# Chunked attention with a channel mix on one Trainium2 core: another way to load and turn the first q and k, three tiles mixed on PE, and a new order of the start

## The chip, the core and the metric

The kernel runs on one core of a Trainium2 chip. Its engines are TensorE (PE), VectorE (DVE), ScalarE (ACT), GpSimd (POOL) and the DMA queues, which SyncE (SP) and ScalarE issue to. The metric is the device time of one execution in microseconds: 616.96 us, the median of three runs (616.75 to 618.72).

## What is computed

The attention works in chunks of 64 tokens, so no chunk sees another one. Its output, 8 batches of 576 tokens of 512 channels, is the x of a channel mix, in which every token is blended with the one before it:

```python
scores = scale * np.matmul(q_c, k_c.transpose(0, 1, 2, 4, 3))   # chunks of 64 tokens, 8 heads of 64
attn = np.exp(scores - max) / (sum + 1e-09)
x = np.matmul(attn, v_c)                                       # to (8, 576, 512)
x_prev = np.concatenate([zeros, x[:, :-1, :]], axis=1)
xk = mu_k * x + (1.0 - mu_k) * x_prev
xr = mu_r * x + (1.0 - mu_r) * x_prev
k = np.maximum(xk @ w_k, 0.0)                                  # 512 -> 1024
v = k * k @ w_v                                                # 1024 -> 512
r = 1.0 / (1.0 + np.exp(-(xr @ w_r)))                          # 512 -> 512
out = r * v
```

q, k and v are float32; the three weight matrices and both mu come from numpy and the weights arrive as 8-byte floats, which the kernel converts on the chip.

## The kernel before

The 4608 tokens are worked in 18 groups of 256 (`G`), a group in two tiles of 128 (`TT`). For a tile, PE forms the scores (task `S`, line 363) from `qT` and `kT`, which hold channels on partitions; DVE and ACT make the softmax; PE turns the probabilities (task `P`, line 420) and multiplies them with v (line 438), which gives x with channels on partitions. Then x is mixed with its shifted self (tasks `Mk` and `Mr`) and split into a high and a low float32r part. For a group PE forms pk in four quarters (task `K`, line 580), pr for two tiles (`R`, line 629) and pv (`V`, line 659), each as three float32r passes (high by high, low by high, high by low). That is 96, 24 and 48 products a group.

From group 3 on q and k come in 32 by 32 blocks, which DVE turns. The first three groups, tiles 0 to 5, are loaded with a token a partition, 256 bytes to a head: `load_nat` issues for each tile and tensor one DMA for each half of the heads (`n` tasks, line 165; four where a tile crosses a batch). PE turns them, four products of 128 by 128 with the identity for a tile and tensor (task `T`, line 318), and ACT or DVE copies the result to `qT` or `kT` (line 131 or 133).

Of these first tiles, 0 to 3 (`ON_PE`, line 474) are mixed on PE: 16 products of x with diagonal matrices of mu and 1 - mu, accumulated (line 528). `make_diag` builds the 16 diagonals on ACT (line 489) from mu, loaded with channels on partitions in runs of 4 bytes (lines 216 and 217). The other tiles are mixed on DVE: a difference, then eight scalar_tensor_tensor instructions (line 540).

The weights come in ten pieces of 1 MB: w_r in two, w_k and w_v in four each. A piece takes two passes on ACT (lines 258 and 262), two on DVE (lines 265 and 271), a copy of the high part (line 131 on ACT or 133 on DVE) and a subtraction for the low part (line 280).

The order of the first two groups is written out by hand: `START` lists steps as task and number, with the engine behind a colon, and each engine and each DMA queue runs its own steps in this order. `W:14` puts 14 products of a zero tile in front of PE (line 723). From group 2 on `GROUP` gives the order. A DMA's end is told by one of eight semaphores, taken in turn, and the DMA that takes a semaphore again first waits for the DMA that had it before; the wait stands in the queue of the engine that issues it.

Of the kernel before, what the change touches and what calls it, by code (L numbers as in the profile page):

```python
# [7 lines left out]
F32 = mybir.dt.float32  # L8
# [3 lines left out]
AF = mybir.ActivationFunctionType  # L12
ALU = mybir.AluOpType
# [65 lines left out]
def tile_chunk_attention_channel_mix(  # L79
# [12 lines left out]
    nc = tc.nc  # L92
# [44 lines left out]
    def queue(e):  # L137
        return nc.scalar if e == "A" else nc.sync
# [7 lines left out]
    def segments(first, many):  # L146

        cut = -first % S
        if 0 < cut < many:
            return [(0, cut), (cut, many - cut)]  # L150
        return [(0, many)]

    def load_nat(t):
        for nm, src in (("q", q), ("k", k)):
            do.task = f"n{nm}{t}"

            def fn(_, nm=nm, src=src):
                g, tl = divmod(t, 2)
                if tl == 0:
                    T[f"{nm}{g}"] = ld.tile([P, 2, HP, 2, D], F32, tag=nm, name=f"{nm}n_{g}")  # L160
                dst = T[f"{nm}{g}"]
                for s, n in segments(t * TT, TT):
                    b, t0 = divmod(t * TT + s, S)
                    for j in range(2):
# [306 lines left out]

    ON_PE = (0, 1, 2, 3)
    diag = {}

    def make_diag():
        do.task = "dg"

        def fn(e):  # L480
            T["diag"] = tmp.tile([P, 4, NB, P], F32, tag="st", name="diag", bufs=1)
            for i, (nm, mu) in enumerate((("k", muk), ("r", mur))):
                rest = const.tile([P, NB], F32, name=f"rest{nm}")
                nc.vector.tensor_scalar(rest, mu, -1.0, 1.0, ALU.mult, ALU.add)
                for n, col in enumerate((mu, rest)):
                    to = diag[nm, n] = T["diag"][:, 2 * i + n]
# [12 lines left out]
    def x_mix(t):
# [16 lines left out]

        do(f_d, "D")
        for nm, mu in (("k", muk), ("r", mur)):

            def f_mix(e, nm=nm, mu=mu):  # L520
                x = xt[t]
                if t in ON_PE:
# [272 lines left out]
```

## Time and profile before

| what | value |
|---|---|
| median of three runs | 616.96 us |
| the profiled execution | 620.49 us, of which the span is 618.7 us |
| PE busy | 601.6 us, 97% |
| DVE busy, ACT busy | 399.8 us, 332.5 us |
| DMA | 49.17 MB, mean 79 GB/s |
| granted PE clock | 0.988 of full speed over the span |

The page cuts the span into 40 slices. PE is busy nine tenths or more from the fifth slice on; in the first four it shows 5, 8, 8 and 8 tenths, the PE clock 9, 7, 9 and 8 tenths. The DMA engines are busiest in those slices. A matmul's end is modelled, so that a lone product looks longer than the distance at which products follow each other. A float32 product with 128 columns stands in the trace as two instructions, a transpose as one.

### The profile page before, as it was taken

What the parts mean: (1) busy time and instruction counts of PE and PEld (TensorE: products, weight loads), DVE (VectorE), ACT (ScalarE), POOL (GpSimd) and SP (SyncE); (2) the same over time, 40 slices, a digit from 0 to 9 for tenths busy, and PEclk for the clock granted to TensorE, in tenths of its full rate; (3) what the DMA queues carried; (4) which work ended last, traced back from release to release, by engine and by line L of the source; (5) the groups of instructions that cost most, each with busy time, mean ns of one, the idle gap of its engine ahead of it and who ended that gap; (6) DMA issues with size and microseconds to landing.
All of it is one profiled execution on the core that took longest, in us unless ns stands there. A gap on an engine that the chain in (4) does not pass through costs nothing.

```text
span 618.7 us, 14035 instructions
## 1 busy us (share of the span) xinstructions
PE 601.6 (97%) x5676; PEld 529.2 (86%) x5676; DVE 399.8 (65%) x860; ACT 332.5 (54%) x519; POOL 0.7 (0%) x6
## 2 busy tenths in 40 slices
PE   5888999999999999999999999999999999999997
PEld 5778988989898989888888888898989898989895
DVE  2767879757666667666666666666766667675610
ACT  4767684454545464646463737372728282827250
POOL 0000000000000000000000000000000000000000
PEclk9798999999999999999999999999999999999999
DMA  8796343244233434242322442234233334020000
GB/s 190 219 280 172 105 109 78 43 88 94 36 56 75 105 70 85 52 90 48 75 52 39 90 98 34 56 79 103 34 62 68 74 77 83 19 57 13 18 18 34
DMA packets 195071, 49.17 MB, mean 79 GB/s; under 512 B 186816, under 2 KB 186816, under 8 KB 195008
## 3 DMA queue, kind: packets, MB, share of 16 engines
q1 hardware_dynamic: 193952, 48.29, 34.9%
q8 instruction: 44, 0.72, 0.5%
q10 hardware_dynamic: 1056, 0.00, 0.1%
q14 instruction: 19, 0.16, 0.1%
HBM read 38.80 MB, written 9.44 MB: 78 GB/s over the span
## 4 chain that ended last, share of the span: by engine, by line
PE 91%; DMA 4%; SPq 3%; DVE 1%; issue 0%; ACT 0%; DVEq 0%
PE pk L580 33%; PE pv L659 33%; PE pr L629 16%; PE xps L438 3%; PE s L363 3%; DMA wk_st<-in_moe_w_k 3%; PE pt L420 2%; SPq L165 2%; SPq L182 1%; DMA wr_st<-in_moe_w_r 1%; PE mxk L528 1%; PE mxr L528 0%; SPq L254 0%; DVE wk_st L265 0%; DVE wk L280 0%
## 5 line engine op out<-in xcount | busy, mean ns | idle before, releaser
L580 PE MATMUL pk<-xkhi,wk 128*128 128x256 f32 x1152 | 217.9, 285 | 1.9 <-DVE wk L133 1.1
L659 PE MATMUL pv<-wv,kk 128*128 128x512 f32 x864 | 205.4, 395 | 0.0
L659 PEld LDWEIGHTS pv<-wv,kk 128*128 128x128 f32 x864 | 161.4, 187 | 39.2 <-DVE wv L280 0.2
L580 PEld LDWEIGHTS pk<-xkhi,wk 128*128 128x128 f32 x1152 | 181.3, 189 | 4.2 <-DVE wk L133 1.3
L580 PE MATMUL pk<-xklo,wk 128*128 128x256 f32 x576 | 162.3, 282 | 0.0
L580 PEld LDWEIGHTS pk<-xklo,wk 128*128 128x128 f32 x576 | 109.3, 190 | 0.9
L594 ACT ACTIVATE relu<-pk 128x512 f32<-128x512 f32 x72 | 42.6, 592 | 99.3 <-PE pk L580 99.3
L613 DVE TENSOR_TENSOR kk<-relu,kk 128x512 fp32r<-128x512 f32 x72 | 49.5, 687 | 69.9 <-ACT kk L131 69.9
L629 PE MATMUL pr<-wr,xrhi 128*128 128x512 f32 x288 | 93.7, 406 | 0.0
L629 PEld LDWEIGHTS pr<-wr,xrhi 128*128 128x128 f32 x288 | 51.4, 188 | 11.0
L629 PE MATMUL pr<-wr,xrlo 128*128 128x512 f32 x144 | 56.8, 395 | 0.0
L373 DVE TENSOR_REDUCE m<-s 128x8 f32<-128x512 f32 x36 | 24.7, 687 | 47.8 <-PE s L363 47.8
L131 ACT ACTIVATE xkhi<-mixk 128x512 fp32r<-128x512 f32 x32 | 20.2, 632 | 58.2 <-DVE mixk L540 58.2
L131 ACT ACTIVATE xrhi<-mixr 128x512 fp32r<-128x512 f32 x31 | 19.6, 632 | 57.0 <-DVE mixr L540 57.0
L131 ACT ACTIVATE kk<-relu 128x512 fp32r<-128x512 f32 x72 | 45.6, 633 | 2.1
L601 ACT ACTIVATE relu<-relu 128x512 f32<-128x512 f32 x72 | 45.5, 632 | 2.1
L540 DVE SCALAR_TENSOR_TENSOR mixk<-d,muk,x 128x128 f32<-128x128 f32 (+1 forms) x144 | 38.5, 332 | 1.0
L540 DVE SCALAR_TENSOR_TENSOR mixr<-d,mur,x 128x128 f32<-128x128 f32 (+1 forms) x144 | 38.3, 331 | 0.0
L559 DVE TENSOR_TENSOR xrlo<-mixr,xrhi 128x512 fp32r<-128x512 f32 x32 | 22.2, 692 | 21.0 <-ACT xrhi L131 21.0
L559 DVE TENSOR_TENSOR xklo<-mixk,xkhi 128x512 fp32r<-128x512 f32 x32 | 22.1, 692 | 20.9 <-ACT xkhi L131 20.9
L672 DVE TENSOR_TENSOR out<-pv,sg 128x512 f32<-128x512 f32 x36 | 24.0, 675 | 16.7 <-PE pv L659 15.7
L131 ACT ACTIVATE pT<-pt 128x512 f32<-128x512 f32 x36 | 21.3, 591 | 22.6 <-PE pt L420 22.6
(75 smaller groups left out, 562.9 us busy)
## 6 DMA issues: line engine op xcount, KB each, us to landing
v<-in_v SPq DMA_DIRECT2D x144, 64.0 KB, 2.5
out<-out SPq DMA_DIRECT2D x36, 256.0 KB, 2.2
q<-in_q SPq DMA_DIRECT2D x160, 32.0 KB, 2.0
k<-in_k SPq DMA_DIRECT2D x160, 32.0 KB, 2.0
wk_st<-in_moe_w_k SPq DMA_DIRECT2D x4, 1024.0 KB, 8.1
wv_st<-in_moe_w_v SPq DMA_DIRECT2D x4, 1024.0 KB, 7.2
wr_st<-in_moe_w_r SPq DMA_DIRECT2D x2, 1024.0 KB, 8.1
qn<-in_q SPq DMA_DIRECT2D x10, 128.0 KB, 2.9
```

The lines of the kernel that those rows point to most:

```text
L131: nc.scalar.activation(to, x, AF.Copy)
L363: nc.tensor.matmul(scores()[halves[e], j, hp, :], qT[halves[j], hp, cols[e]], kT[halves[j], hp, cols[e]], start=True, stop=True,)
L373: nc.vector.tensor_reduce(out=heads(m), in_=scores(), axis=AX.X, op=ALU.max)
L540: nc.vector.scalar_tensor_tensor(out=m[:, cb, s : s + w], in0=d[:, cb, s : s + w], scalar=mu[:, cb : cb + 1], in1=x[:, cb, c : c + w], op0 ...
L559: engine[e].tensor_tensor(lo[:, :, part], T[f"m{nm}{t}"], hi[:, :, part].bitcast(F32), ALU.subtract)
L580: nc.tensor.matmul(pk[:, e, :], wk[a][:, cb, f * P : (f + 1) * P], xk[b][:, cb, :], start=(n == 0), stop=(n == 3 * NB - 1),)
L594: nc.scalar.activation(r, T[f"pk{g}{fp}"], AF.Relu)
L601: nc.scalar.activation(r, r, AF.Square)
L613: engine[e].tensor_tensor(lo, T[f"r{g}{fp}"], hi.bitcast(F32), ALU.subtract)
L629: nc.tensor.matmul(pr, xr[a][:, cb, tl * TT : (tl + 1) * TT], wr[b][:, cb, :], start=(n == 0), stop=(n == 3 * NB - 1),)
L659: nc.tensor.matmul(T[f"pv{g}{tl}"], kk[a][:, f, tl * TT : (tl + 1) * TT], wv[b, f // 4][:, f % 4, :], start=(f == 0 and n == 0), stop=(f = ...
L672: nc.vector.tensor_tensor(o, T[f"pv{g}{tl}"], T[f"sg{g}{tl}"], ALU.mult)
```

## The change

First, the natural loads. `load_nat` now takes a whole group: partition p holds tokens 2p and 2p + 1, 512 bytes to a head, all eight heads in one DMA of 512 KB (two for group 2, which crosses a batch). q and k of tiles 0 to 5 are 8 DMAs in place of 28. The turn is now by parity r: for each r and tensor eight products, each of one head (64 columns of the stationary operand) with the identity, head j * 4 + hp into half j of the output partitions. It is an ordinary float32 product, not a transpose. The copy writes every second column of `qT` or `kT`.

Second, mu is loaded as rows of 128 (4 rows each, 512 bytes), turned by one PE product and moved by two ACT instructions, which also make 1 - mu. Its DMAs are issued from ACT's queue.

Third, `ON_PE` is 0 to 2; tile 3 is mixed on DVE. The diagonals, d and the mixes share one ring of four buffers.

Fourth, `START` is another list. `W:14` becomes `W:9` at the front, `W:4` behind the first turns, `W:4` and `W:3` around the first turn of group 1. One piece of w_r is issued from ACT's queue at the very start. In `GROUP` two neighbours change places.

```diff
 START = """
-W:14 Mk3.0:D nq0.0 nk0.0 T0.2 T0.0 T0.3:D mu.0:A T0.1:D Mk0.0:D nq1.0 P0.3:D nk1.0 T1.0 S0.0
+W:9 Mk2.0:D nk0.0 T0.6 nq0.0 T0.4 swr1.0:A T0.7:A P0.3:D T0.5:A T0.0 T0.2 T0.1:A mu.0 nk1.0
+T0.3:A W:4 S0.0 cwr1.0:A mu.1 S1.0 S0.1:D W:4 T1.4 S0.2:D S0.3:A mu.2:A S1.1:D T1.5:A nq1.0 W:3
...
-    def load_nat(t):
+    def load_nat(g):
...
-                        nc.sync.dma_start(
-                            out=dst[s : s + n, tl, :, j, :],
-                            in_=src[b, j * HP : (j + 1) * HP, t0 : t0 + n, :].rearrange(
-                                "h p d -> p h d"
-                            ),
-                        )
+                dst = T[f"{nm}{g}"] = ld.tile([P, H, 2, D], F32, tag=nm, name=f"{nm}n_{g}")
+                for s, n in segments(g * G, G):
+                    b, t0 = divmod(g * G + s, S)
+                    nc.sync.dma_start(
+                        out=dst[s // 2 : (s + n) // 2, :, :, :],
+                        in_=src[b, :, t0 : t0 + n, :].rearrange("h (p r) d -> p h r d", r=2),
+                    )
...
-            queue(e).dma_start(out=muk, in_=mu_k.rearrange("(c p) -> p c", p=P))
-            queue(e).dma_start(out=mur, in_=mu_r.rearrange("(c p) -> p c", p=P))
+            for i, mu in enumerate((mu_k, mu_r)):
+                queue(e).dma_start(
+                    out=mus[i * NB : (i + 1) * NB], in_=mu.rearrange("(c p) -> c p", p=P)
+                )
+
+        def f_tr(_):
+            T["mu"] = ps_k.tile([P, 2 * NB], F32, tag="k", name="mu_t")
+            nc.tensor.transpose(out=T["mu"], in_=mus, identity=ident[: 2 * NB, : 2 * NB])
+
+        def f_move(e):
+
+            x = T["mu"].rearrange("p (i c) -> p i c", i=2)
+            nc.scalar.activation(mu2[:, 0], x, AF.Copy)
+            nc.scalar.activation(mu2[:, 1], x, AF.Copy, scale=-1.0, bias=1.0)
...
-                x = T[f"tr{nm}{t}"] = ps_k.tile([P, HP, TT], F32, tag="k", name=f"tr{nm}_{t}")
-                for hp in range(HP):
-                    nc.tensor.transpose(
-                        out=x[:, hp, :],
-                        in_=T[f"{nm}{g}"][:, tl, hp],
-                        identity=ident,
-                    )
-
-            def f_move(e, nm=nm, to=to):
-                copy(e, to[:, :, tl * TT : (tl + 1) * TT], T[f"tr{nm}{t}"])
+            for r in range(2):
+
+                def f_tr(_, nm=nm, r=r):
+                    x = T[f"tr{nm}{r}{g}"] = ps_k.tile([P, HP, P], F32, tag="k", name=f"tr{nm}{r}_{g}")
+                    for hp in range(HP):
+                        for j in range(2):
+                            nc.tensor.matmul(
+                                x[halves[j], hp, :],
+                                T[f"{nm}{g}"][:, j * HP + hp, r, :],
+                                ident,
+                                start=True,
+                                stop=True,
+                            )
+
+                def f_move(e, nm=nm, to=to, r=r):
+                    copy(e, to.rearrange("p h (c r) -> p h r c", r=2)[:, :, r, :], T[f"tr{nm}{r}{g}"])
...
-    ON_PE = (0, 1, 2, 3)
+    ON_PE = (0, 1, 2)
...
-            T["diag"] = tmp.tile([P, 4, NB, P], F32, tag="st", name="diag", bufs=1)
+                    to = diag[nm, n] = mo.tile([P, NB, P], F32, tag="mix", name=f"diag_{nm}{n}", bufs=4)
```

How the order moves is shown at three places. PE at the start of the program, before (`trk` and `trq` are turns of k and q, `s` scores, `pt` turned probabilities, `xps` the x of a tile, `warm` the zero products):

```order
L723 MATMUL warm<-idle 128x128 x14
L318 MATMUL trk_129<-ident,kn_126 128x128 x4
L318 MATMUL trq_134<-ident,qn_123 128x128 x4
L318 MATMUL trq_149<-ident,qn_123 128x128 x4
L363 MATMUL s_154<-kT,qT 64x64 x16
L318 MATMUL trk_208<-ident,kn_126 128x128 x4
L363 MATMUL s_154<-kT,qT 64x64 x16
```

And now:

```order
L731 MATMUL warm<-idle 128x128 x9
L328 MATMUL trk_0_120<-ident,kn_118 64x128 x8
L328 MATMUL trk_0_131<-ident,kn_118 64x128 x8
L328 MATMUL trq_0_146<-ident,qn_129 64x128 x8
L328 MATMUL trq_0_155<-ident,qn_129 64x128 x8
L731 MATMUL warm<-idle 128x128 x4
L375 MATMUL s_174<-kT,qT 64x64 x16
L218 MATMUL mu_t<-ident,mus 128x8
L375 MATMUL s_174<-kT,qT 64x64 x16
L731 MATMUL warm<-idle 128x128 x4
L328 MATMUL trk_1_216<-ident,kn_167 64x128 x8
L731 MATMUL warm<-idle 128x128 x3
```

Both scores of group 0 now stand behind all four of its turns, and the idle products stand in three more places. ACT at the start, before, with the semaphores that it waits for (`DMAHW` are those of the DMAs):

```order
L216 DMA muk<-in_moe_mu_k 128x4x1
L217 DMA mur<-in_moe_mu_r 128x4x1
L489 ACT_TABLE_LOAD [waits DMAHW0_49]
L489 ACTIVATE diag<-ident,muk 128x128 [waits Pool_49]
L489 ACTIVATE diag<-ident,muk 128x128 x3
```

And now:

```order
L263 DMA wr_st<-in_moe_w_r 128x2x1024
L132 ACT_TABLE_LOAD
L132 ACTIVATE kT<-trk_0_120 128x512 [waits PE_49]
L132 ACTIVATE kT<-trk_0_131 128x512 [waits PE_49]
L132 ACTIVATE qT<-trq_0_146 128x512 [waits PE_49]
L212 DMA mus<-in_moe_mu_k 4x128 [waits DMAHW5_49]
L212 DMA mus<-in_moe_mu_r 4x128 [waits DMAHW7_49]
L132 ACTIVATE qT<-trq_0_155 128x512 [waits PE_49]
```

The diagonals have left ACT's start, the four copies of group 0 stand there, and the loads of mu stand ahead of the last of these copies; semaphores 5 and 7 were last taken by the first and the third piece of v of tile 0. The DMAs that SP issues first, before:

```order
L165 DMA qn_123<-in_q 128x4x64 x2
L165 DMA kn_126<-in_k 128x4x64 x2
L165 DMA qn_123<-in_q 128x4x64 x2
L165 DMA kn_126<-in_k 128x4x64 x2
L254 DMA wr_st<-in_moe_w_r 128x2x1024
L182 DMA v_196<-in_v 64x4x64 x4
L165 DMA kn_203<-in_k 128x4x64 x4
```

And now:

```order
L162 DMA kn_118<-in_k 128x8x128
L162 DMA qn_129<-in_q 128x8x128
L162 DMA kn_167<-in_k 128x8x128
L162 DMA qn_233<-in_q 128x8x128
L177 DMA v_269<-in_v 64x4x64 x3
L177 DMA v_269<-in_v 64x4x64 [waits DMAHW0_49]
L263 DMA wr_st<-in_moe_w_r 128x2x1024 [waits DMAHW1_49]
L162 DMA kn_296<-in_k 32x8x128 [waits DMAHW2_49,PE_49]
```

q and k of two groups now go ahead of everything else on SP's queue, in four DMAs.

## Rows read from the trace of the kernel before

**Rows 1.** Busy time by stretch (windows, in us from the span's start: length, then PE, PE's weight loads, DVE, ACT and POOL busy with their instruction counts, PE clock, DMA share, GB/s), the span cut where the products become continuous and where the last one ends.

```profile
0.00:60.00 60.00, 46.78 (x572) 42.09 (x573) 37.55 (x56) 40.75 (x65) 0.70 (x6) 0.89 0.83 219
60.00:614.88 554.88, 554.79 (x5107) 487.13 (x5105) 361.53 (x804) 291.76 (x455) 0.00 (x0) 1.00 0.31 64
614.88:618.70 3.82, 0.00 (x0) 0.00 (x0) 0.69 (x1) 0.00 (x0) 0.00 (x0) 0.81 0.18 69
```

**Rows 2.** The same columns, with the first 60 us cut where the granted PE clock changes.

```profile
1.05:6.26 5.21, 5.21 (x24) 5.21 (x25) 0.00 (x0) 2.56 (x5) 0.25 (x1) 1.00 0.90 178
13.09:23.33 10.24, 7.03 (x85) 5.95 (x86) 8.08 (x13) 7.68 (x13) 0.00 (x0) 0.50 0.78 205
54.05:57.46 3.41, 3.19 (x15) 3.19 (x16) 3.38 (x5) 1.58 (x2) 0.00 (x0) 0.50 0.29 47
```

**Rows 3.** The waits of PE in the first 60 us, longest first (in all, times, longest, us).

```profile
PE s L363 <- ACT kT L131: 4.9, 1, 4.9
PE xps L438 <- ACT pT L131: 2.3, 2, 1.6
PE pk L580 <- DVE wk L133: 1.1, 1, 1.1
PE s L363 <- DVE p L379: 0.9, 1, 0.9
PE pk L580 <- DVE wk L280: 0.8, 1, 0.8
PE pt L420 <- DVE p L379: 0.7, 1, 0.7
```

**Rows 4.** The chain that ended last, in order of time, three stretches (start, us, what, count): the two mixes of tile 3, the turn between the K products and the scores of a group, and the end.

```profile
66.84 1.78 PE mxk L528 x16
68.63 1.79 PE mxr L528 x16
...
143.95 2.84 PE pk L580 x24
146.79 1.09 PE s L363 x64
147.88 5.88 PE pk L580 x48
153.76 0.44 PE pt L420 x4
...
597.99 5.60 PE pr L629 x24
614.88 0.69 DVE out L672
```

**Rows 5.** Timeline (start, us, engine, line, operation): the idle products at the start on PE; ACT's first diagonals, its copy ahead of the second scores, and those scores; and the first K product.

```profile
1.05 5.86 PE L723 MATMUL warm<-idle 128*128 128x128 f32 x28 [1.05 <-DVE idle L121]
4.75 1.28 ACT L489 ACTIVATE diag<-ident,muk 128x128 f32<-128x128 f32 x4
...
14.34 0.57 ACT L131 ACTIVATE kT<-trk 128x512 f32<-128x512 f32 x1
14.96 1.13 PE L363 MATMUL s<-kT,qT 64*64 64x64 f32 x32 [4.95 <-ACT kT L131]
...
47.52 0.37 PE L580 MATMUL pk<-xkhi,wk 128*128 128x256 f32 x1
```

**Rows 6.** Windows again (columns as rows 1) in which the DMA queues moved runs of one size almost alone: 256 B (q and k), 4 KB (w_r), 2 KB (w_k).

```profile
4.00:6.00 2.00, 2.00 (x11) 2.00 (x11) 0.00 (x0) 1.99 (x5) 0.00 (x0) 1.00 1.06 238
17.00:19.00 2.00, 1.23 (x5) 0.72 (x4) 1.97 (x3) 0.69 (x2) 0.00 (x0) 0.50 0.96 350
25.00:27.00 2.00, 2.00 (x23) 1.88 (x20) 1.90 (x2) 1.97 (x5) 0.00 (x0) 1.00 1.03 391
```

**Rows 7.** DMA issues of two windows (0.7 to 5.05 us, and 5.05 to 5.6 us): line, queue, count, KB each, median us from issue to landing.

```profile
qn<-in_q SPq DMA_DIRECT2D x4, 128.0 KB, 2.8
...
wr_st<-in_moe_w_r SPq DMA_DIRECT2D x1, 1024.0 KB, 8.3
```

**Rows 8.** Windows of 10 us from the start (columns as rows 1).

```profile
0.00:10.00 10.00, 8.60 (x76) 7.89 (x76) 1.98 (x5) 2.56 (x5) 0.70 (x6) 1.00 0.85 210
10.00:20.00 10.00, 3.72 (x57) 2.81 (x60) 6.89 (x13) 8.35 (x19) 0.00 (x0) 0.65 0.85 213
20.00:30.00 10.00, 9.11 (x156) 8.45 (x152) 7.44 (x12) 8.04 (x13) 0.00 (x0) 0.83 0.76 208
30.00:40.00 10.00, 8.94 (x95) 8.19 (x87) 9.26 (x16) 6.39 (x10) 0.00 (x0) 1.00 0.90 224
50.00:60.00 10.00, 7.99 (x134) 7.24 (x133) 9.78 (x10) 7.93 (x12) 0.00 (x0) 0.83 0.56 130
```

**Rows 9.** Groups of instructions in the first 80 us (busy us, mean ns of one, idle before): the steps that make a w_k quarter usable, and the mix on DVE over the whole run.

```profile
L262 ACT ACTIVATE wk_st<-wk_st 128x1024 int32<-128x1024 uint32 x4 | 4.5, 1134 | 4.7 <-DMA wk_st<-in_moe_w_k 4.7
L265 DVE SCALAR_TENSOR_TENSOR wk_st<-wk_st 128x1024 int32<-128x1024 int32 x4 | 4.9, 1220 | 5.7 <-ACT wk_st L258 5.7
L280 DVE TENSOR_TENSOR wk<-wk_st,wk 128x1024 fp32r<-128x1024 f32 x4 | 4.9, 1226 | 2.3 <-ACT wk L131 2.1
...
L540 DVE SCALAR_TENSOR_TENSOR mixk<-d,muk,x 128x128 f32<-128x128 f32 (+1 forms) x144 | 38.5, 332 | 1.0
```

More of the change, by code (lines that the diff above doesn't have):

```diff
@@ new lines @@
+Mr1.1:A T2.2 Mk1.1 hwr0.0:A Mr1.2:D cwk0.1:A S3.5:D cwk0.0:D hwr0.1:D cwk0.2:D P2.2 cwk0.3:D
+T2.3:A T2.7:A P3.0 P3.1:A Mk1.2:A hwk0.0:D cwk2.0:A T2.0 swv0.0 cwk2.1:A Mk1.3:D R00.0 P2.4:A
+hwk0.1:D cwk3.1:A cwk1.0:D v3.0 cwk2.2:D cwk3.0:A R01.0 cwk2.3:D K00.0 R00.1:A cwk3.2:D Mr2.0
+T2.1:A P3.3:D cwk1.2:D R01.1:A hwk2.0:A swv1.0 K00.1:A P3.2 cwk1.3:D Mr2.1:A hwk2.1:D cwk3.3:D
+v4.0 P3.4:A Mk2.1 hwk1.0:A K00.2:A Mk3.0:D bq3.0 hwk1.1:D hwk3.0:A hwk3.1:D K02.0 cwv2.1:A
+K02.1:A K00.3:A cwv1.1:A Mr2.2:D S4.0 K01.0 K03.0 Mr3.0:D cwv2.0:A R10.0 Mr3.1:A Mk3.1:D
@@ new lines @@
+cwv2.2:D cwv0.0:A cwv2.3:D cwv0.1:A hwv2.0:A S4.1:D Mk2.2:A Mr3.2:D Mk3.2:A S5.0 K02.2:A
+K02.3:A K00.4:D Mk2.3:D v5.0 R10.1:A Mk3.3:D R11.0 S4.2:D K02.4:D hwv2.1:D cwv0.2:D K01.1:A
+K01.2:A K01.3:A cwv0.3:D K03.1:A K10.0 cwv1.0:A Mk0.0:D K03.2:A swv3.0 K11.0 bk3.0 S5.1:D
+R11.1:A K01.4:D cwv1.2:D cwv1.3:D bq4.0 hwv0.0:A K10.1:A hwv0.1:D K12.0 V001.0 S4.3:A cwv3.1:A
+V001.1 S5.2:D S4.4:D hwv1.0:A S4.5:D cwv3.0:A K03.3:A hwv1.1:D P4.0 P4.3:D cwv3.2:D V001.2
+P4.1:A cwv3.3:D S5.3:A K10.2:A K10.3:A hwv3.0:A K03.4:D V001.3 K10.4:D K11.1:A hwv3.1:D P4.2
@@ L56 @@
 Lq K0.0 Sa.0 Sb.0 Sa.12 K0.123 Sa.3 Sb.12 K0.4 Sb.3 Sa.45 Sb.45 K1 K2.0 Pa.0 K2.1234 Pa.1
-K3.0 Pb.0 Pb.1 K3.1234 Tc R0 Pa.2 Pb.2 Pa.34 Pb.34 Lv Lk Mka R1 Mkb Mra Mrb Td V0 V1
+K3.0 Pb.0 Pb.1 K3.1234 Dc R0 Pa.2 Pb.2 Pa.34 Pb.34 Lv Lk Mka R1 Mra Mkb Mrb Dd V0 V1
 """
@@ L125, in tile_chunk_attention_channel_mix @@
     make_identity(nc, ident)
-    muk = const.tile([P, NB], F32, name="muk")
-    mur = const.tile([P, NB], F32, name="mur")
+    mus = const.tile([2 * NB, P], F32, name="mus")
+    mu2 = const.tile([P, 2, 2, NB], F32, name="mu2")
+    muk, mur = mu2[:, 0, 0], mu2[:, 0, 1]
     def copy(e, to, x):
@@ L151, in segments @@
         return [(0, many)]
-    def load_nat(t):
+    def load_nat(g):
         for nm, src in (("q", q), ("k", k)):
-            do.task = f"n{nm}{t}"
+            do.task = f"n{nm}{g}"
             def fn(_, nm=nm, src=src):
[L158 to L164, printed above, removed]
-                        nc.sync.dma_start(
-                            out=dst[s : s + n, tl, :, j, :],
-                            in_=src[b, j * HP : (j + 1) * HP, t0 : t0 + n, :].rearrange(
-                                "h p d -> p h d"
-                            ),
-                        )
+                dst = T[f"{nm}{g}"] = ld.tile([P, H, 2, D], F32, tag=nm, name=f"{nm}n_{g}")
[5 more added lines that the diff above has]
+                    )
             do(fn, "Q")
@@ L334, in att_qk @@
         part = slice(tl * TT, (tl + 1) * TT)
-        do.task = f"T{t}"
+        do.task = f"D{t}"
         for nm, to in (("q", qT), ("k", kT)):
@@ L480, in fn @@
         def fn(e):
-            T["diag"] = tmp.tile([P, 4, NB, P], F32, tag="st", name="diag", bufs=1)
[L482 to L486, printed above, removed]
+            for i, nm in enumerate("kr"):
+                for n in range(2):
+                    to = diag[nm, n] = mo.tile([P, NB, P], F32, tag="mix", name=f"diag_{nm}{n}", bufs=4)
                     for cb in range(NB):
+                        col = mu2[:, n, i, cb : cb + 1]
                         if e == "A":
-                            nc.scalar.activation(
-                                to[:, cb], ident, AF.Copy, scale=col[:, cb : cb + 1]
-                            )
-                        else:
-                            nc.vector.tensor_scalar(
-                                to[:, cb], ident, col[:, cb : cb + 1], None, ALU.mult
-                            )
+                            nc.scalar.activation(to[:, cb], ident, AF.Copy, scale=col)
+                        else:
+                            nc.vector.tensor_scalar(to[:, cb], ident, col, None, ALU.mult)
         do(fn, "D")
@@ L506, in f_d @@
                 return
-            d = T[f"d{t}"] = mo.tile([P, NB, TT], F32, tag="d", name=f"d_{t}", bufs=2)
+            d = T[f"d{t}"] = mo.tile([P, NB, TT], F32, tag="mix", name=f"d_{t}", bufs=4)
             x = xt[t]
@@ L535, in f_mix @@
                     return
-                m = T[f"m{nm}{t}"] = mo.tile([P, NB, TT], F32, tag="mix", name=f"mix{nm}_{t}")
+                m = T[f"m{nm}{t}"] = mo.tile([P, NB, TT], F32, tag="mix", name=f"mix{nm}_{t}", bufs=4)
                 d = T[f"d{t}"]
@@ L681, in tile_chunk_attention_channel_mix @@
     for t in range(6):
-        load_nat(t)
+        if t % 2 == 0:
+            load_nat(t // 2)
         load_v(t)
@@ L698, in tile_chunk_attention_channel_mix @@
     for t in range(6):
-        move_qk(t)
+        if t % 2 == 0:
+            move_qk(t // 2)
         att_scores(t)
```

47 lines of the change are left out of this document (17 added, 30 removed).

## The prediction

> **What bounds the kernel now.** I read the windows of the span first, then the chain of waits, PE's waits, and the DMA rows. From 60 us to 614.88 us PE is busy for 554.79 of 554.88 us [rows 1], so there every microsecond of PE work is one of time, and nothing that DVE, ACT or the DMAs do shows. All slack stands in the first 60 us: PE is busy for 46.78 of them [rows 1]. The idle products take 5.86 us of that [rows 5], and two stretches run at half the granted clock, with 7.03 and 3.19 us of PE work in them [rows 2], of which half, 5.1 us, would not be there at full clock. (The stretch from 1.05 us prints a clock of 1.00, but nothing ran in it except idle products, 28 instructions in 5.86 us or 209 ns each, where a mix product takes 1.78 / 16 = 111 ns [rows 2, 4, 5].)
>
> So I keep a ledger. The last product ends at 614.88 us; 3.82 us of tail follow [rows 1], which the change leaves alone. PE's work at full clock is 46.78 + 554.79 - 5.86 - 5.1 = 590.6 us. The rest, 614.88 - 590.6 = 24.3 us, is lost time: 13.3 us idle, 5.9 us of idle products, 5.1 us of half clock. The idle time is 4.9 us before the second scores of group 0, 3.9 us on links of its softmax and values (2.3 + 0.9 + 0.7), 1.9 us for w_k before the second K product (1.1 + 0.8) [rows 3], and small pieces.
>
> **The change part by part.** *Tile 3's mixes* leave PE: 1.78 + 1.79 = 3.57 us less work [rows 4]. On DVE they cost a difference and eight instructions of 332 ns [rows 9], about 3.3 us, when DVE is at its fullest: 9.78 of 10 us between 50 and 60 us [rows 8]. Their reader is pk of group 1, several K, R and mix steps behind; that work covers it, and without the cover it would cost those 3.3 us.
>
> *The turns.* There are 12 steps before and after (three groups, q and k, two halves or two parities). Before, a step is four transposes, 0.44 us by the same shape in the chain [rows 4]. Now a step is eight float32 products, so 16 instructions of 128 columns on 64 columns of the array. At 111 ns each they take 1.78 us if the two halves never run together and 0.89 us if they always do. The trace shows no half-array product; the nearest row is the scores, which use quarters: 64 instructions of 64 columns in 1.09 us, 17 ns each, against 111 / 2 = 55.5 ns on the whole array [rows 4]. So 3.3 of 4 quarters run at once, 82%. I take 82% of two halves: 16 x 111 / 1.64 = 1.08 us a step, 12 x 0.64 = 7.7 us more PE work, with bounds of 5.4 and 16.1 us.
>
> PE's work after is 590.6 - 3.6 + 7.7 = 594.7 us. With the same end the lost time could be 614.88 - 594.7 = 20.2 us. The change therefore has to save 4.1 us of lost time before it gains anything.
>
> *The loads, and when the first scores start.* A DMA of 128 KB landed 2.8 us after its issue [rows 7]; 0.55 us of that is transfer at 238 GB/s [rows 6], so 2.25 us are fixed. The trace has no run of 512 B: 256 B went at 238 GB/s, 2 KB at 391 [rows 6]; I take the middle, 310, since 512 lies as near to one as to the other. The second copy of q stands on ACT behind both loads of mu, and the second of these waits for the third piece of v. Ahead of that piece go 2.10 MB of q and k (6.8 us), 1.05 MB of w_r from ACT's queue (3.0 us at 350 GB/s [rows 6]) and 0.2 MB of v (0.8 us): it lands at 0.74 + 2.25 + 10.6 = 13.6 us. The load of mu (0.5 us to issue) and a copy of 0.57 us [rows 5] bring the scores to 14.8 us. Against this, w_r took 8.3 us to land [rows 7], 3 us longer than 2.25 + 3.0; if this lateness falls ahead of v, 17.8 us. PE would have done its four turns and idle products by 13 to 15 us. I take 15.5 us, nearer to the early end because w_r now runs on its own queue. Behind these waits on ACT stand the conversion of w_r and the first exp; both need data that is late anyway. The second scores follow at once, where before they started at 14.96 us [rows 5]: what was a wait for kT behind the diagonals becomes a wait for qT behind mu.
>
> The Trainium skill, "DMA: Bandwidth & Descriptors", section Specifications, gives 512 B as the least run that goes at line rate. By it q and k would need 2.10 MB at 391 GB/s, 1.4 us less, which lies inside the rival of better loads; no run here shows it.
>
> *The idle products.* Nine in front (before: 14) stand inside the wait for the first k. The four before the scores are covered too. The seven behind them are 14 instructions, 1.55 us at full clock, on PE's path. What they may save is half clock: before, 7.03 / 2 = 3.5 us between 13 and 23 us [rows 2]. I allow 1.0 us of half clock after the scores, between none and 3.5.
>
> *The softmax links* of tiles 0 and 1 lost 3.9 us before [rows 3]. Their waits stay; the diagonals, four of them 1.28 us [rows 5], 16 of them 5.1 us, now stand on ACT behind the first x and ahead of tile 2's exp, while PE has the turns of group 1, scores and values to do. I take 3.5 us (2.5 to 4.5).
>
> *The weights.* Up to the first K product PE has 12 turns (13.0 us), four scores (2.2), four turned probabilities (1.8), three values (1.6, at the price of scores), four mixes (7.1) and pr (5.6): 31.3 us, each at its row [rows 4]. With 17.3 us lost it starts at 48.6 us, 1.1 us later than the 47.52 of before [rows 5]. The w_k piece for it needs two passes on ACT, two on DVE, a copy and a subtraction, 1.13 to 1.23 us each [rows 9], 7.1 us, so it has to land by 41.5 us. Up to it 8.1 MB are queued; before, 8.55 MB had moved by 40 us (210, 213, 208 and 224 GB/s [rows 8]). So the weights are covered by about 3 us even at the old pace, and the 1.9 us wait for the second piece goes, with its 1.6 us of half clock. What is late next is the last q of group 2, queued behind v of tile 2, whose buffer PE frees with the first values; I leave 0.5 us for it.
>
> **The sum.** Lost time: 15.5 - 4 x 1.08 = 11.2 us up to the scores, 1.55 for idle products, 3.5 for links, 1.0 for half clock, 0.5 later: 17.75 us. The span is 594.7 + 17.75 + 3.82 = 616.3 us, 2.4 us under 618.7. The profiled execution took 620.49 us, 3.5 above the median; on the median the same difference gives 614.5 us. With the softer bounds of these terms it lies between 611.5 and 617 us.
>
> **The rivals.**
> *The loads do better.* Halves run together (0.89 us a step), scores at 14.8 us, links at 2.5 us, no half clock: work 592.4, lost 11.2 + 1.55 + 2.5 = 15.3 us, span 611.5, on the median 609.8 us. For it speaks that bubbles in the queue fill with 512 KB DMAs; against it that all ends are good at once.
> *The first loads come late.* w_r's lateness falls ahead of v, scores at 17.8 us: 2.3 us more, 616.8 us, no change. For it the 8.3 us of w_r; against it the separate queue.
> *The halves do not run together.* A step is 1.78 us. Four steps in a row on PE, from 7 us, with the idle products, put the scores at about 17 us. Work 603.1, lost 9.9 + 1.55 + 3 + 1 + 0.5 = 16 us, span 622.9, on the median 621.2: slower. It decides from about 1.08 + 2.4 / 8 = 1.4 us a step, as eight steps stand on the path. For it: quarters differ in rows and in columns, halves in columns alone, so the scores do not show which of the two overlaps. Against it: with rows alone only two of four quarters could run at once, and 3.3 do.
> *Turning the array over costs.* In the steady part 48 K products around a turn to scores take 5.88 us, where 2 x 2.84 is 5.68 [rows 4]: 0.2 us a turn at most. At 12 new half-array steps that is 2.4 us, and the gain is gone: 616.9 us, no change. The Trainium skill, "TensorEngine Tiling (Array Packing)", section Key Properties, says that a change of tiling mode drains TensorE. The trace agrees only as far as these 0.2 us.
>
> **How the numbers follow.** Forecast 0.42, better loads 0.13, late loads 0.17, halves apart 0.20, turning cost 0.08. No change means within 0.3%, 1.85 us of 616.96, about what a measurement of this kernel can tell. Of the forecast's chance a good three quarters lies below 615.1 us; with nearly all of the better loads and some of the small rivals that is 0.50 faster. The late loads, the turning cost and the forecast's upper end give 0.25 for no change; halves apart and the tails of late loads 0.25 slower. The range from 609.8 to 620.8 us reaches to the better loads and near the halves apart.
>
> **What would show it.** Right: a turn step near 1.1 us; scores of group 0 near 15.5 us, the wait before them ended by ACT's copy of q; about 9 us of PE idle time before 60 us; no wait for w_k before K products and no half clock around 54 us; PE without gaps from about 30 us on. Wrong: a step of 1.4 us or more; first scores after 18 us; a half clock that lasts beyond 25 us, each microsecond of work in it costing another half; or waits for w_k after 50 us, which would mean that the conversions on DVE, not the loads, had become the bound.

## The result and the profile after

The changed kernel takes 621.94 us (median of 17 runs, 620.64 to 622.79), the kernel before 618.72 us (17 runs). Medians here and below take in every run, ratios leave out slow ones (one of 734.16 us here, one of 834.98 us with w_r behind). The ratio is 1.0055, with a 95% interval from 1.0039 to 1.0072: slower, by about 3.4 us, where 2.4 us less was forecast. The profiled execution took 621.98 us, of which the span is 619.9 us. (That of before, 620.49 us, lay 1.8 us above the larger sample's median, so the two traces differ by less than the medians.)

Windows of the changed kernel, columns as in [rows 1]; they answer to [rows 1, 2]:

```profile
0.00:60.00 60.00, 49.33 (x636) 44.00 (x637) 34.29 (x51) 39.38 (x66) 0.70 (x6) 0.91 0.81 235
60.00:616.22 556.22, 556.21 (x5167) 487.96 (x5165) 364.04 (x811) 296.22 (x461) 0.00 (x0) 1.00 0.30 63
616.22:619.90 3.68, 0.00 (x0) 0.00 (x0) 0.69 (x1) 0.00 (x0) 0.00 (x0) 0.96 0.19 71
...
8.59:12.01 3.42, 3.42 (x37) 3.42 (x35) 0.00 (x0) 1.26 (x2) 0.00 (x0) 0.50 1.22 289
18.83:25.66 6.83, 5.48 (x58) 4.81 (x59) 3.93 (x8) 0.91 (x4) 0.00 (x0) 0.50 0.66 187
54.05:57.46 3.41, 3.41 (x30) 3.37 (x29) 3.04 (x5) 3.38 (x6) 0.00 (x0) 1.00 1.08 305
```

From 60 us on PE is full, as before. The stretch around 54 us has the whole clock now; a new half clock stands at 18.83 to 25.66 us. PE's waits in the first 66 us, against [rows 3]:

```profile
PE mu_t L218 <- DMA mus<-in_moe_mu_r: 4.4, 1, 4.4
PE trk L328 <- DMA kn<-in_k: 2.4, 1, 2.4
PE mxk L534 <- DVE xrlo L565: 1.0, 1, 1.0
PE s L375 <- ACT qT L132: 0.9, 1, 0.9
PE s L375 <- DVE m L385: 0.8, 1, 0.8
```

The longest is a wait that the kernel before does not have: the small product that turns mu waits for its load. The chain (start, us, what) shows what it holds up, and where the weights begin:

```profile
9.91 4.15 DMA v<-in_v
...
14.09 5.96 DMA mus<-in_moe_mu_r
20.18 0.24 PE mu_t L218
20.43 1.06 PE s L375 x32
21.49 2.00 PE warm L731 x8
...
48.60 5.79 PE pr L635 x24
54.39 2.84 PE pk L586 x24
```

The first scores had run at 15.08 us. The second ones, behind mu on PE, start at 20.36, and DVE begins its first max only then. The timeline has both (PE, then DVE, whose first 20 us are idle), and a pair of turn steps at full clock:

```profile
15.08 0.69 PE L375 MATMUL s<-kT,qT 64*64 64x64 f32 x32 [0.93 <-ACT qT L132]
20.18 0.24 PE L218 MATMUL mu_t<-ident,mus 8*128 8x8 f32 x1 [4.41 <-DMA mus<-in_moe_mu_r]
20.36 1.13 PE L375 MATMUL s<-kT,qT 64*64 64x64 f32 x32
26.34 1.97 PE L328 MATMUL trq<-ident,qn 128*64 128x128 f32 x32
...
21.55 0.69 DVE L385 TENSOR_REDUCE m<-s 128x8 f32<-128x512 f32 x1 [20.55 <-PE s L375]
```

Why does a load of 2 KB take 5.96 us? Before, the loads of the two mu were the first that ACT issued (DMA issues from 0.7 to 3.5 us: count, KB, us to landing):

```profile
muk<-in_moe_mu_k ACTq DMA_DIRECT2D x1, 2.0 KB, 2.7
mur<-in_moe_mu_r ACTq DMA_DIRECT2D x1, 2.0 KB, 3.0
```

Now they stand behind the third copy of group 0 and are issued at 13.45 and 14.09 us, when 1 MB of w_r, 512 KB of k and a piece of v have just been issued on SP's queue. The DMA queues of the changed kernel (q1 is SP's, q10 ACT's; packets, MB, share), first from 14.4 to 18.0 us, then from 18.0 to 18.7:

```profile
q1 hardware_dynamic: 966, 1.10, 105.9%
...
q1 hardware_dynamic: 398, 0.14, 119.3%
q10 hardware_dynamic: 16, 0.00, 4.1%
```

Not one packet of ACT's queue moves up to 18.0 us, though both loads of mu were issued on it by 14.36 us. Their 16 packets move between 18.0 and 18.7 us, and the load counts as landed at 20.05.

### The profile page after: what moved, and what is told of

Its sections match the earlier page's. It is cut to its first block, busy times and chain, and to the rows that moved or that the text cites. A ratio compares the mean times of both kernels' runs of the same rounds, so it can differ in the third digit from the quotient of the medians.

```text
span 619.9 us, 14270 instructions
## 1 busy us (share of the span) xinstructions
PE 605.5 (98%) x5801; PEld 532.0 (86%) x5801; DVE 399.0 (64%) x862; ACT 335.6 (54%) x526; POOL 0.7 (0%) x6
## 4 chain that ended last, share of the span: by engine, by line
PE 94%; DMA 2%; ACT 2%; SPq 1%; DVE 1%; issue 0%; DVEq 0%
PE pk L586 34%; PE pv L665 33%; PE pr L635 17%; PE xps L450 3%; PE s L375 3%; PE pt L432 3%; SPq L162 1%; DMA mus<-in_moe_mu_r 1%; DMA v<-in_v 1%; PE mxk L534 1%; PE warm L731 0%; PE trq L328 0%; PE trk L328 0%; ACT diag_k L499 0%; SPq L177 0%; ACT diag_r L499 0%
## 5 line engine op out<-in xcount | busy, mean ns | idle before, releaser
L132 ACT ACTIVATE xrhi<-mixr 128x512 fp32r<-128x512 f32 x33 | 20.9, 633 | 48.9 <-DVE mixr L546 48.9
L546 DVE SCALAR_TENSOR_TENSOR mixk<-d,mu,x 128x128 f32<-128x128 f32 (+1 forms) x148 | 39.7, 333 | 1.0
L546 DVE SCALAR_TENSOR_TENSOR mixr<-d,mu,x 128x128 f32<-128x128 f32 (+1 forms) x148 | 39.5, 332 | 0.0
```

What stands on the lines that cost most here:

```text
L132: nc.scalar.activation(to, x, AF.Copy)
L546: nc.vector.scalar_tensor_tensor(out=m[:, cb, s : s + w], in0=d[:, cb, s : s + w], scalar=mu[:, cb : cb + 1], in1=x[:, cb, c : c + w], op0 ...
```

## The experiments

Theory M was that mu's late landing, with its product ahead of the second scores, is the loss. The rivals were the added work of the turns and idle products (W), and a start that is bounded by something further on, so that a wait taken away comes back (R). Each ratio is to runs of the kernel before that were taken along with the variant; their medians lie between 617.08 and 618.88 us, so two variants can differ by up to 1.8 us more or less in their times than in their ratios.

**Mu's product later.** Loads as they are; the product and the two moves stand behind the second turn of group 1.

```diff
-S0.0 cwr1.0:A mu.1 S1.0 S0.1:D W:4 T1.4 S0.2:D S0.3:A mu.2:A S1.1:D T1.5:A nq1.0 W:3
-T1.2 S1.2:D S1.3:A
...
+S0.0 cwr1.0:A S1.0 S0.1:D W:4 T1.4 S0.2:D S0.3:A S1.1:D T1.5:A nq1.0 W:3
+T1.2 mu.1 S1.2:D S1.3:A
...
+T1.3:A mu.2:A T1.1:A
```

> The changed kernel with one edit: the product that turns mu, and ACT's two moves of it, stand behind the second turn of group 1 instead of between the two scores of group 0. The loads are issued as before. Theory M (the late landing of mu, 20.05 us, holds up the second scores, the first max and all that follows): the second scores start at 15.8 us, the first max at about 16.6 us instead of 21.55, the wait of 4.4 us goes and part of the half clock after 18.8 us with it; 4.4 to 7 us less than the changed kernel's 621.9 us, so 615 to 617.5 us, under the kernel before. Rival R (the start is bounded by what comes behind, the conversions on ACT and DVE or the loads of group 2, so that the wait moves there): within 1.5 us of 621.9. Rival W (the added work of the turns and the idle products is the loss, and mu only fills a gap that exists anyway): within 1.5 us of 621.9 as well, with new waits of PE for the softmax or v between 16 and 30 us.

Measured: 616.21 us (ratio to before 0.9982, 0.9965 to 1.0), 5.7 us less than the changed kernel (4.5 us by the ratios). Its timeline (the scores are one run of 64 now):

```profile
14.91 1.16 PE L375 MATMUL s<-kT,qT 64*64 64x64 f32 x64 [0.87 <-ACT qT L132]
20.01 0.22 PE L218 MATMUL mu_t<-ident,mus 8*128 8x8 f32 x1
21.13 1.09 PE L328 MATMUL trq<-ident,qn 128*64 128x128 f32 x16 [0.90 <-ACT mu L223]
```

Its window up to the first pr product (columns as in [rows 1]):

```profile
0.00:42.46 42.46, 35.17 (x538) 31.45 (x538) 23.56 (x40) 28.02 (x52) 0.70 (x6) 0.96 0.87 258
```

and the same for the changed kernel:

```profile
0.00:48.60 48.60, 37.93 (x538) 33.88 (x538) 23.64 (x40) 28.01 (x52) 0.70 (x6) 0.89 0.77 226
```

The same 538 products end 6.14 us earlier: PE is idle for 42.46 - 35.17 = 7.29 us instead of 10.67 (the 4.4 us, less 0.9 us of a new wait for the moves of mu, and small pieces), and busy for 2.76 us less, which is work that had stood at half clock. M holds, W and R fall. From the first pr product to the end the spans are equal: 619.9 - 48.60 = 571.3 us and 613.7 - 42.46 = 571.2. All that this edit did is decided before that product.

**The first max ahead of the second scores**, the other thing that came late on DVE.

```diff
-mu.1 S1.0 S0.1:D
+mu.1 S0.1:D S1.0
```

> The changed kernel with one edit on DVE's order: the first max stands ahead of the second scores of group 0, so that it runs at about 16 us instead of 21.55; mu stays late and its product stays between the scores. If the place of the max, and not mu, was the loss: 616 to 618 us. Theory M: the subtraction behind the max still waits for the second scores, and PE, which is busy from 20.4 to 31 us with turns and idle products, does not come to the turned probabilities earlier: 620.5 to 622 us, no change.

Measured: 621.66 us, ratio 1.0054 (1.0038 to 1.007): no change, although the first max runs 5.6 us earlier:

```profile
15.91 0.69 DVE L385 TENSOR_REDUCE m<-s 128x8 f32<-128x512 f32 x1 [14.90 <-PE s L375]
```

Mu is the cause, and DVE's late start one of its effects.

**Mu loaded first.**

```diff
-W:9 Mk2.0:D nk0.0 T0.6 nq0.0 T0.4 swr1.0:A T0.7:A
+W:9 Mk2.0:D nk0.0 T0.6 nq0.0 T0.4 mu.0 swr1.0:A T0.7:A
```

> The changed kernel with one edit: the two loads of mu are the first DMAs that ACT issues, ahead of w_r; the product on mu stays between the scores. Theory M: mu lands within some 3 to 4 us, its product does not wait, and the last copy of q on ACT, which waited behind the issue of mu, is free as well (scores 0.5 to 1 us earlier than 15.08): 5 to 8 us less than 621.9, 614 to 617 us. Rivals R and W: within 1.5 us of 621.9. w_r on ACT's queue starts 0.8 us later; it landed at 6.9 us and its first use is at 14.9, so nothing from that.

Measured: 612.39 us, ratio 0.992 (0.9897 to 0.9942), 9.5 us less than the changed kernel (8.3 us by the ratios) and faster than the one before. That is more than expected. Its timeline says why:

```profile
5.19 2.89 PE L328 MATMUL trk<-ident,kn 128*64 128x128 f32 x32
9.53 1.97 PE L328 MATMUL trq<-ident,qn 128*64 128x128 f32 x32 [1.45 <-DMA qn<-in_q]
11.43 1.16 PE L731 MATMUL warm<-idle 128*128 128x128 f32 x8
12.51 0.69 PE L375 MATMUL s<-kT,qT 64*64 64x64 f32 x32
13.14 0.22 PE L218 MATMUL mu_t<-ident,mus 8*128 8x8 f32 x1
```

No wait for mu; and the first turns start at 5.19 us, not 7.67: w_r, issued 0.9 us later, no longer takes the DMA engines from the first k. The queues show it (packets, MB, share), first the changed kernel from 3.5 to 5.5 us, then this run from 2 to 5 us:

```profile
q10 hardware_dynamic: 169, 0.69, 85.5%
q1 hardware_dynamic: 170, 0.09, 15.3%
...
q1 hardware_dynamic: 1510, 0.76, 98.0%
q10 hardware_dynamic: 16, 0.03, 3.2%
```

In the changed kernel the two queues move as many packets, but those of w_r hold 4 KB and those of k 512 bytes, so that k and q get 0.09 of 0.78 MB. (The traced run with mu first took 614.0 us, the longest of its six; it has a half clock from 24.19 to 27.61 us, and the other five, 612.31 to 612.53 us, a granted clock of 0.999 or 1.0 over the span.)

**Mu second.** The same, with w_r ahead of mu at the head of ACT's queue, to part the two.

```diff
-T0.4 mu.0 swr1.0:A T0.7:A
+T0.4 swr1.0:A mu.0 T0.7:A
```

> The changed kernel with one edit, as in the run with mu first, but the loads of mu stand behind that of w_r at the head of ACT's queue. It separates two things that the run with mu first changed together: mu landing before its use (4.4 us of wait, the issue on ACT out of the way of the last copy of q, the clock), and w_r issued 0.9 us later, so that the first k landed at 5.0 us instead of 7.5. If the first alone made the gain (theory M): 612.5 to 613.5 us. If the place of w_r made a part of it (theory Q: what the first k waits for on the DMA engines): the first k lands at about 7.5 us as in the changed kernel, scores at about 14 us instead of 12.5, and the time is 1.5 to 2.5 us above that run, 614 to 615 us.

Measured: 615.6 us, ratio 0.9971 (0.9954 to 0.9987), a little above its range.

```profile
7.98 3.68 PE L328 MATMUL trk<-ident,kn 128*64 128x128 f32 x32 [2.72 <-DMA kn<-in_k]
...
15.24 0.69 PE L375 MATMUL s<-kT,qT 64*64 64x64 f32 x32
15.86 0.22 PE L218 MATMUL mu_t<-ident,mus 8*128 8x8 f32 x1
```

PE does not wait for mu here either, but for the first k. So mu's part is about 6.3 us by the medians (5.2 by the ratios), and the place of w_r is a second loss of the changed kernel: the sum had 3.0 us for w_r ahead of v, and nothing for what it does to the first k. Its size is less sure: 3.2 us by the medians, but the runs with mu second spread from 613.9 to 616.9 us, and why was not found.

**W_r behind the first k and q.** The run with mu first, w_r's early piece on SP's queue.

```diff
-T0.4 mu.0 swr1.0:A T0.7:A ... T0.1:A nk1.0
+T0.4 mu.0 T0.7:A ... T0.1:A swr1.0 nk1.0
```

> The run with mu first, with the early piece of w_r on SP's queue behind the first k and q instead of on ACT's own queue. Theory Q (what shares the DMA engines with the first q and k sets when the scores start): the first q lands at about 7.5 us instead of 9.4, the scores start at 10.5 to 11 us instead of 12.5, w_r lands at about 10 us, ahead of its use: 2 us less than 612.4, 610.0 to 611 us. Rival S (the softmax and v, or DVE and ACT, which are busy for 9 of 10 us from 20 us on, set the time by then): 611.5 to 613 us.

Measured: 611.66 us, ratio 0.9881 (0.9855 to 0.9908). The scores come at 10.06 us, 2.45 us earlier, as theory Q has it, but by the medians only 0.7 us is left of it at the end. PE's first products behind tile 2's max:

```profile
21.65 0.69 PE L375 MATMUL s<-kT,qT 64*64 64x64 f32 x32 [1.63 <-DVE m L385]
22.27 1.90 PE L328 MATMUL trk<-ident,kn 128*64 128x128 f32 x16
24.10 1.13 PE L450 MATMUL xps<-pT,v 64*64 64x64 f32 x32
```

Behind the wait for tile 2's max the clock is at half, from 22.40 to 25.81 us: 1.90 us for a turn of 1.09, 1.13 for values of 0.69. The traced run with mu first has the same wait (1.62 us) and as long a half clock behind it, and against that trace the gain is whole: the first pr product starts at 38.21 us instead of 40.62, and 611.84 us stand against 614.0. Of its six runs only this one was so; with w_r behind, three of five have a granted clock of 0.997 (611.49 to 611.84 us), two of 0.999 or 1.0 (610.73 and 611.53). The medians fall to rival S, but that the half clock is what took the gain is not shown.

**The idle products** behind the scores away: from the changed kernel, and from the one with mu first.

```diff
-W:4 T1.4
+T1.4
...
-W:3
```

> The changed kernel without the seven idle products behind the scores of group 0 (2.07 + 1.08 us in the trace, the first four at half clock). Theory M: PE runs on to the turned probabilities, which are ready at about 26.1 us, so at most 2.2 us of the 3.15 come back: 619.7 to 621 us; if the clock stays at half for longer without them, the gain is gone: 621.5 to 623 us. Rival W: the full 3.15 us, 618.8 us.

> The run with mu first, without the seven idle products behind the scores (1.16 + 0.94 us, at full clock there). Theory A (they stand on PE's path): the turned probabilities of tile 0 are ready at 18.56 us and PE comes to them at 18.79, so PE would then wait for the softmax: at most 0.3 us less, 612.1 us. Theory C (they keep the clock up): a stretch at half clock between 14 and 25 us, 613 to 615 us.

Measured: 620.36 us (ratio 1.005, 1.0032 to 1.0068) and 612.52 us (0.9929, 0.991 to 0.9949): both ratios lie within the intervals of the kernels that have them. With mu first PE meets the same softmax a little earlier and waits:

```profile
16.28 1.97 PE L328 MATMUL trq<-ident,qn 128*64 128x128 f32 x32 [1.31 <-ACT mu L224]
18.58 0.65 PE L432 MATMUL pt<-ident,p 128*128 128x128 f32 x4 [0.33 <-DVE p L405]
```

There they cost nothing and give nothing. In the changed kernel it stays open: by the medians 1.6 us came back, as theory M has it, by the ratios 0.3.

**The old loads and turns**, in the new order with mu first: a token a partition, 128 KB a DMA, four transposes a step.

```diff
-dst = T[f"{nm}{g}"] = ld.tile([P, H, 2, D], F32, tag=nm, name=f"{nm}n_{g}")
+dst = T[f"{nm}{g}"] = ld.tile([P, 2, HP, 2, D], F32, tag=nm, name=f"{nm}n_{g}")
...
+nc.tensor.transpose(out=x[:, hp, :], in_=T[f"{nm}{g}"][:, r, hp], identity=ident)
```

> The run with mu first, with the loads and turns of q and k as in the kernel before (a token a partition, 128 KB a DMA, four transposes a step) in the new order. A step is 0.44 us instead of 0.985, 16 more DMAs to issue. Theory W (the added work of the turns counts where PE does not wait): the eight steps behind the first scores give 8 x 0.545 = 4.4 us, 608 to 609 us, if the loads land as before; those of 256 B runs are slower, so that the first scores come 1 to 2 us later: 609 to 611 us. Rival L (the loads of two tokens a partition are worth their turns): the scores come over 4 us later, or waits for q and k of group 1 and 2 appear: above 612.4 us.

Measured: 615.58 us, ratio 0.9983 (0.9965 to 1.0001), 3.2 us more than with the new ones.

```profile
PE trk L332 <- DMA kn<-in_k: 3.7, 1, 3.7
PE trq L332 <- DMA qn<-in_q: 3.0, 1, 3.0
PE trq L332 <- ACT qT L132: 1.9, 1, 1.9
```

By its steps PE has 12 x 0.545 = 6.5 us less to do, and it waits for the loads instead, for the first k and for q of group 2. (The traced run, 618.1 us, is the longest of twelve.) Rival L holds for this order, which was written for the new loads: two tokens a partition pay for the dearer turns. Loads and turns changed together here; a variant with the new loads and four whole transposes a step gave no result, so what each does alone is not shown.

**Tile 3 on PE**, with mu first.

```diff
-    ON_PE = (0, 1, 2)
+    ON_PE = (0, 1, 2, 3)
```

> The run with mu first, with tile 3 mixed on PE again (and one subtraction on DVE put ahead of the other mix, which shares its buffer ring). The prediction took 3.57 us off PE's work for tile 3 and nothing for its nine instructions on DVE: by that 616.0 us. If DVE, which is busy for over 9 of 10 us there, pays for it elsewhere: less than 2 us more, below 614.5.

Measured: 620.39 us, ratio 1.0054 (1.0033 to 1.0074): 8.0 us more, above both of its ranges. (One subtraction on DVE moves ahead of a mix as well.) Besides the two mixes PE waits, where with mu first it did not at all after 39 us:

```profile
PE mxk L534 <- DVE xklo L565: 1.7, 1, 1.7
PE pr L635 <- DVE xrlo L565: 1.4, 1, 1.4
PE pr L635 <- DVE xklo L565: 0.8, 1, 0.8
```

3.57 + 3.9 = 7.5 us. The 3.9 belong to this order, which was written for mixes on DVE.

**Together.** All edits that seemed to help, then two variants that keep the idle products and the second scores' place, and let steps of w_r on DVE follow tile 2's max and subtraction: three steps, or all of them but `cwr1.3:D`. The edit for three, on the kernel with w_r behind:

```diff
-nk2.0 cwr1.3:D T1.7:A P1.0 P0.2 hwr1.0:D P1.1:A S2.0 P0.4:A v1.0 S2.1:D S3.0
-T2.4 hwr1.1:D S2.2:D
+nk2.0 T1.7:A P1.0 P0.2 P1.1:A S2.0 P0.4:A v1.0 S2.1:D S3.0
+T2.4 S2.2:D cwr1.3:D hwr1.0:D hwr1.1:D
```

> All that seems to help at once: mu first, the early piece of w_r on SP's queue behind the first k and q, no idle products behind the scores, the first max ahead of the second scores, and the max and subtraction of tile 2 ahead of three of w_r's steps on DVE (the wait of 1.6 us for that max). Theory Q: 1 to 2 us less than the run with w_r behind, 608.5 to 610 us. Rival S: within 1 us of 612.4; a half clock after the scores without idle products would cost 1 to 2 us.

> The run with w_r behind, with three of w_r's steps on DVE behind the max and subtraction of tile 2 (PE's wait for that max was 1.63 us, and the clock went to half right behind it). If the wait and the half clock that follows it cost what the rows say: 0.8 us of the wait, and up to 1.7 us of half clock, 609.0 to 611.0 us. If DVE, moved work and all, hands the wait on to the mixes (a wait for xr's low part, 0.9 us in the run with everything at once): 611 to 612 us.

> The same with only one of the three steps moved (the copy of w_r's high part), so that the two passes of w_r stay ahead of the max: a wait of about 1.0 us instead of 1.63. Gain of half the other, 610 to 611.7 us.

Measured: 611.24 us (0.988, 0.9854 to 0.9907), 611.05 us (0.9887, 0.9863 to 0.9911) and 611.04 us (0.9885, 0.9863 to 0.9907). The first missed its range. The others lie 0.6 us under the kernel with w_r behind by the medians, not under it by the ratios (its own is 0.9881): no gain is shown. The clock stays whole in the last, and its first pr product, by the chain, is the earliest of the variants:

```profile
37.41 5.79 PE pr L635 x24
```

To the end of its span of 608.7 us that is 571.3 us again. It beats both kernels; the edits that do it are the two places in the DMA queues.

## Why the prediction was wrong

*The place of mu was the step that failed.* "The second scores follow at once" did not hold: the prediction charged the load of mu with 0.5 us to issue, ahead of the last copy of q, and did not ask when it lands, although the order rows beside it show the mu product between the two scores. It landed at 20.05 us. With the product moved back, PE is idle for 3.4 us less and, with less work at half clock, busy for 2.8 us less: the 6.1 us of the first experiment.

*The rest of the sum, against the trace.* PE's work: 49.33 + 556.21 = 605.5 us busy, less 8.5 us of idle products (4.21, 1.16, 2.07, 1.08), less half of the 3.42 and of the 5.48 - 2.07 us at half clock, 3.4: 593.6 us, where 594.7 was forecast. The difference is the turn step: 1.97 / 2 = 0.985 us, not 1.08, so 12 x 0.095 = 1.1 us. The halves do run together, and neither that rival nor the cost of turning the array over shows. Lost time: 616.22 - 593.6 = 22.6 us instead of 17.75; without mu's 4.4 it would be 18.2.

*First scores*: 15.08 us for 15.5, the wait ended by ACT's copy of q behind the third piece of v, which landed at 14.06 us for 13.6: as forecast. But the queue of its own, taken as a help, did not keep w_r out of the way of the first k: with mu first, and then with w_r behind, the scores start at 12.51 and 10.06 us. The rival of late loads had this piece, at the wrong place.

*The idle products* were charged with 1.55 us. With mu first they are free, since PE waits for the softmax without them; in the changed kernel their price is open (0.3 to 1.6 us). *Half clock after the scores*: 1.0 us allowed; (5.48 - 2.07) / 2 = 1.7 us in the trace, and it goes with mu. *Softmax links*: 3.5 us allowed for tiles 0 and 1; no wait of PE for their softmax stands in the trace. The waits behind it are 0.8 us for tile 2's max and 1.0 us at a mix.

*Tile 3*: the rows bear out 3.57 us off PE and no wait for DVE in its place; taken back onto PE in this order it costs more than double. *The weights*: right, no wait for w_k and no half clock at 54 us. The first K product came at 54.39 us instead of 48.6, and the 5.8 us between them are nearly the 6.1 that mu cost.

*Bandwidth.* The prediction took 310 GB/s for runs of 512 B. Between 7 and 9 us, when q and k moved alone, and for 1 us of the run with w_r behind, when they moved almost alone:

```profile
7.00:9.00 2.00, 1.32 (x21) 1.36 (x23) 0.00 (x0) 0.15 (x1) 0.00 (x0) 0.90 1.22 294
...
3.30:4.30 1.00, 1.00 (x7) 1.00 (x6) 0.00 (x0) 0.00 (x0) 0.00 (x0) 1.00 1.16 344
```

The rule of the Trainium skill, "DMA: Bandwidth & Descriptors", section Specifications, that 512 B is enough for line rate, would have had 391 here, if the rate at 2 KB [rows 6] is taken for line rate. The measurement decides against it: 294 GB/s in the changed kernel, and 344 in the other run.

With mu's product out of the way (616.21 us) the kernel is no slower than the one before, and 1.7 us above the forecast; with its loads moved up behind w_r (615.6 us) it is 0.3% faster (0.9954 to 0.9987). What goes beyond that, and beyond the forecast, came with the place of w_r.

## What to carry to other kernels

A load is not costed by its issue: follow it to its landing, and count what was issued shortly before it on every queue. Here 2 KB behind 1.6 MB landed 6 us after their issue; before, as the first loads, it was 3 us. Of two loads that start together, look at the packets: the one with short packets got the small share of the bytes. A small product that needs such a load does not belong between two steps of the critical path on an engine that works in order. Where an order is new, go down each engine's list once and ask of every row when its data lands, also of rows that take 0.2 us.

## What the runs showed of the hardware

Two queues that both move share the DMA engines by packets, not by bytes. W_r, issued on ACT's queue at 0.73 us, and k, issued on SP's at 0.74, moved 169 and 170 packets from 3.5 to 5.5 us, but 0.69 and 0.09 MB. K's turns began at 7.67 us, and at 5.19 when w_r was issued 0.9 us later. The Trainium skill, "DMA: Bandwidth & Descriptors", section "Queues, rings and completion order", says that each DMA engine takes turns between the queues with work, packet by packet; this stretch agrees, with one run of 4 KB or 512 bytes to a packet.

A load issued later on the other queue did not take its turn at once. Mu's 16 packets, issued on ACT's queue at 13.45 and 14.09 us, stood still until 18.0 us, while SP's queue moved 1.10 MB from 14.4 us on. With mu first, w_r, issued at 1.62 us behind k, moved at most 0.03 MB from 2 to 5 us, while SP's queue moved 0.76. If these packets had been ready at the engines, taking turns would have moved them sooner; where they waited was not tried.

Half-array products overlap, close to two at a time: 16 instructions of 128 columns in 0.985 us, 62 ns each, against 111 ns on the whole array [rows 4].
